# The second layer's pairs in a written order, with a second stage of seven block products

## The chip, the cores and the metric

The kernel runs on one core of a Trainium2 chip. The metric is the device time of one execution in microseconds (us); the time before is the median of three runs, 1736.29 us (1735.03 to 1740.18). The core has five instruction streams that matter here: TensorE (PE) multiplies, VectorE (DVE) and ScalarE (ACT) do elementwise work, GpSimd (POOL) helps in the attention layers, and SyncE (SP) issues the DMA transfers.

## What is computed

Four layers with residuals are applied to x, 2048 rows of 640 numbers: attention over a dilated window (layer A), a Fourier mixing layer (layer B), and both again.

```python
x = x + A(layernorm(x), wqkv, wo)
x = x + B(layernorm(x), seq_re, seq_im, hid_re, hid_im)
x = x + A(layernorm(x), wqkv, wo)
x = x + B(layernorm(x), seq_re, seq_im, hid_re, hid_im)

def B(x, Cr, Ci, Hr, Hi):      # 2048x2048 and 640x640
    a = x @ Hr.T
    b = x @ Hi.T
    return Cr @ a - Ci @ b
```

Only layer B is touched by the change, and above all its second use.

## The kernel before

Layer B is computed in the other order. The first stage multiplies the normalised x with the sequence matrices and gives, for a tile of 256 output rows, a real part Zr and an imaginary part Zi, held transposed: five chunks of 128 hidden columns, each with 256 rows of Zr and 256 of Zi. The second stage is y = Zr Wr + Zi Wi (the sign is in Wi), with contraction over the five chunks. There are eight such tiles, t = 0 to 7.

Every fp32 operand is split in a high part and the rest (hi and lo, both float32r), and every product is three matmuls (hi hi, hi lo, lo hi; `PASSES`). Splitting a coefficient tile (`s_split`) is a ScalarE copy (line 1327) and a VectorE subtraction (line 1328).

Tiles 1 to 6 are made in three pairs (`pair`, t1 = 2p + 2 and t2 = 2p + 3) that take seven block products in place of eight in the first stage. A pair is three sweeps over eight steps i. A step loads coefficient tiles of 128 x 512 numbers (256 KB; `s_raw`, line 1317) into seven buffers in turn (five of tag win, two of xa), forms sums and differences of them on VectorE (`combine`, line 1363), splits them into six split buffers (`views`), loads ready-made combinations of x (256 KB; `x_slot`, line 1307) into slots, and multiplies (`product`, line 1334). A block product of a step is six matmuls of 512 columns, a product with the fifth chunk three. So the first sweep has 18 matmuls and two x loads a step (m5, m4, m7), the second 21 and two (m2, f1, f2, f1, m1), the third 15 and one (m3, f2, m6). There are eight x slots in the first two sweeps and four in the third. Between the sweeps VectorE and ScalarE combine the eight PSUM banks' results into the pair's two tiles, `zt_put` splits a tile into four buffers (lines 1207, 1209, 1212), and `ymm` (line 1233) does the second stage for a row block of 128: per chunk and half of 320 columns, three passes for each of Zr and Zi, 60 matmuls for a row block and 120 for a tile. The row blocks of tile 2p + 1 stand at the end of the first and the second sweep, the first one of t1 inside the third sweep (12 matmuls a step from the fourth step on), its second one at the third sweep's end. Tiles 0 (in `run`) and 7 (after the last pair) are done apart. `yout` loads the residual rows, adds the two halves (line 1246) and stores (line 1253).

What sets the order: on TensorE it is the order in which the program is written, in both layers. The other engines of the pairs, SP's queue among them, are ordered by a scheduler that may move an instruction ahead of others that are written before it. Whatever stands behind a waiting instruction on one engine, or behind a waiting transfer on SP's queue, waits with it. `run` comes ahead of the pairs of each layer B: it does the first stage of tile 1, loads and splits the second stage's weights (`load_w`: wr and wi), and stores the combinations of x to DRAM (`x_combine`). In the first layer B the third pair is interleaved with the start of the next attention layer and has only the win buffers from its fourth step on.

## Time and profile before

| | before |
|---|---|
| median of three runs | 1736.29 us |
| profiled execution, first to last instruction | 1734.8 us |
| TensorE busy | 1715.3 us, 99% |
| VectorE busy | 1355.3 us, 78% |
| ScalarE busy | 824.7 us, 48% |
| DMA traffic | 419.91 MB, mean 242 GB/s |

The profiled execution has no time of its own but the span between its first and its last instruction, 1734.8 us; the median of the timed runs is 1.49 us above that span. The page of the profile gives busy time by engine and by groups of equal instructions. The chain of work that ended last follows the program back from its end, at each step to what released it. The waits list who stood idle until whom. In a window the columns are busy time of each engine with the number of its instructions, the granted clock of TensorE (1.00 is full), the share of the 16 DMA engines in use and the rate. In that profile layer B's pairs stand at about 457 to 868 us (first) and 1314 to 1707 us (second), each pair taking 133.3 us; the program ends with the second stage of the last tiles.

### The profile page before, as it was taken

The page shows a single profiled execution, that of the slowest core. Times are in us where ns is not written, and L with a number is a line of the kernel's source. Part 1 is how long each engine was busy: PE and PEld are TensorE (multiplying, and loading weights), DVE is VectorE, ACT ScalarE, POOL GpSimd, SP SyncE. Part 2 cuts the span into 40 slices and gives each one's busy share as a digit, 9 for nine tenths or more (in the row PEclk, how much of TensorE's full clock was granted, in tenths as well). Part 3 has the DMA queues.
Part 4 walks back from the last instruction along what each step waited for, and adds up shares of the span by engine and source line. Part 5 has one row for each costly group of instructions (what it writes and reads, how often), then busy time and mean ns, then how long its engine had stood idle before and what let it go on. Part 6 is the DMA issues. An engine that isn't in the chain of part 4 may idle for free.

```text
span 1734.8 us, 26552 instructions
## 1 busy us (share of the span) xinstructions
PE 1715.3 (99%) x8825; PEld 1496.1 (86%) x8825; DVE 1355.3 (78%) x2118; ACT 824.7 (48%) x1815; POOL 616.4 (36%) x570
## 2 busy tenths in 40 slices
PE   9999999999999999999999999999999999999999
PEld 7888888878888888888888889888888888888888
DVE  5999999978768667668639998899787677686673
ACT  5655645655445444445534434555444443443441
POOL 3899999940000000000019997899200000000000
PEclk9999999999999999999999999999999999999999
DMA  7768678959787687687547856698597867767761
GB/s 248 259 226 260 215 241 307 335 192 355 258 268 239 221 258 227 218 268 227 186 156 259 281 165 223 214 338 282 195 345 258 264 204 259 256 209 244 261 203 54
DMA packets 266713, 419.91 MB, mean 242 GB/s; under 512 B 22192, under 2 KB 144560, under 8 KB 266320
## 3 DMA queue, kind: packets, MB, share of 16 engines
q1 hardware_dynamic: 252400, 408.55, 71.2%
q10 hardware_dynamic: 14176, 9.67, 1.8%
q8 instruction: 70, 1.15, 0.3%
q14 instruction: 67, 0.55, 0.1%
HBM read 332.99 MB, written 85.14 MB: 241 GB/s over the span
## 4 chain that ended last, share of the span: by engine, by line
PE 86%; DVE 5%; POOL 3%; DMA 2%; issue 2%; ACT 2%; SPq 0%; DVEq 0%; ACTq 0%; POOLq 0%
PE m L499 18%; PE aux L1233 16%; PE t L1334 11%; PE m L1334 11%; PE aux L662 6%; PE pq L1334 6%; PE xt L1334 5%; PE m L1166 4%; PE t L1166 4%; PE xt L1166 2%; DVE pr L579 2%; DVE pr L622 1%; POOL pr L637 1%; POOL pr L582 1%; POOL pr L638 1%
## 5 line engine op out<-in xcount | busy, mean ns | idle before, releaser
L499 PE MATMUL m<-r,s 128*128 128x512 f32 (+1 forms) x1890 | 421.8, 378 | 0.2 <-ACT sg L514 0.2
L499 PEld LDWEIGHTS m<-r,s 128*128 128x128 f32 x1890 | 344.5, 188 | 54.7 <-ACT sg L514 1.6
L1327 ACT CAST r<-win 128x512 fp32r<-128x512 f32 x242 | 147.4, 621 | 168.2 <-DVE win L1363 80.4
L1233 PE MATMUL aux<-r2a,zo 128*128 128x320 f32 x768 | 226.0, 309 | 0.0
L579 DVE TENSOR_TENSOR pr<-pq,win 128x1280 f32<-128x1280 f32 x128 | 189.8, 1483 | 37.2 <-PE aux L1233 20.3
L637 POOL TENSOR_TENSOR pr<-pr 128x640 f32<-128x640 f32 x126 | 207.7, 1648 | 27.1 <-DVE pr L622 25.9
L1233 PE MATMUL aux<-pr,zo 128*128 128x320 f32 x704 | 208.0, 309 | 0.0
L582 POOL TENSOR_TENSOR pr<-pr 128x640 f32<-128x640 f32 x123 | 176.6, 1436 | 87.6 <-DVE pr L579 87.6
L622 DVE TENSOR_TENSOR pr<-pq,win 128x1280 f32<-128x1280 f32 x128 | 190.3, 1488 | 2.6
L1328 DVE TENSOR_TENSOR r<-win,r 128x512 fp32r<-128x512 f32 x242 | 162.7, 687 | 37.8 <-ACT r L1327 36.5
L300 POOL TENSOR_TENSOR stats<-stats,mhalf 128x1 f32<-128x1 f32 (+1 forms) x26 | 18.9, 728 | 445.9 <-ACT stats L294 445.9
L1334 PE MATMUL m<-r,r 128*128 128x512 f32 x600 | 153.0, 389 | 0.5 <-DVE r L1328 0.5
L1233 PEld LDWEIGHTS aux<-r2a,zo 128*128 128x128 f32 x768 | 144.1, 188 | 2.2
L1233 PEld LDWEIGHTS aux<-pr,zo 128*128 128x128 f32 x704 | 132.2, 188 | 2.4
L1334 PEld LDWEIGHTS m<-r,r 128*128 128x128 f32 x600 | 112.4, 188 | 24.0 <-DVE r L1328 1.0
L1334 PE MATMUL t<-r,r 128*128 128x512 f32 x492 | 132.0, 390 | 0.0
L638 POOL TENSOR_TENSOR pr<-pr 128x320 f32<-128x320 f32 x126 | 113.0, 897 | 9.9
L592 DVE TENSOR_REDUCE lg<-pr 128x64 f32<-128x640 f32 (+1 forms) x128 | 107.2, 837 | 11.4 <-POOL pr L582 11.3
L1363 DVE TENSOR_TENSOR win<-win,win 128x512 f32<-128x512 f32 x109 | 74.9, 691 | 49.9 <-DMA win<-cs_in 48.4
L1334 PEld LDWEIGHTS t<-r,r 128*128 128x128 f32 x492 | 92.4, 188 | 19.8
L1166 PE MATMUL m<-s,r 128*128 128x512 f32 x348 | 106.8, 395 | 1.7 <-ACT r L1103 0.9
L1166 PE MATMUL t<-s,r 128*128 128x512 f32 x348 | 105.2, 390 | 0.0
(299 smaller groups left out, 3245.6 us busy)
## 6 DMA issues: line engine op xcount, KB each, us to landing
win<-cs_in SPq DMA_DIRECT2D x346, 256.0 KB
r<-xc SPq DMA_DIRECT2D x240, 256.0 KB
win<-kvb SPq DMA_DIRECT2D x96, 440.0 KB
xa<-cs_in SPq DMA_DIRECT2D x120, 256.0 KB
win<-kvb SPq DMA_DIRECT2D x64, 360.0 KB
xc<-sg SPq DMA_DIRECT2D x28, 512.0 KB
xr<-xs SPq DMA_DIRECT2D x40, 320.0 KB
kvb<-stg SPq DMA_DIRECT2D x33, 320.0 KB
```

Of the source, the lines that this page charges most:

```text
L499: nc.tensor.matmul(mt[g][:, : GW[q]], st[:, a, k], wq[q][:, b, k], start=n == 0, stop=n == 14)
L579: nc.vector.tensor_tensor(pr, q, wview(u, jp, 0, [[1, FE]]), op=ALU.mult)
L582: nc.gpsimd.tensor_tensor(pv[:, :, 0:10], pv[:, :, 0:10], pv[:, :, 10:20], op=ALU.add)
L592: nc.vector.tensor_reduce(rows(lgs[u], jp), pv.rearrange("p (a h) d -> p a h d", h=HE), axis=AX.X, op=ALU.add,)
L622: nc.vector.tensor_tensor(pr.rearrange("p j w (h d) -> p (j w) h d", d=DH), rows(lgs[u], jp).unsqueeze(3).to_broadcast([P, 2 * W, HE, DH]) ...
L637: g.tensor_tensor(pr[:, :, 0:4], pr[:, :, 0:4], pr[:, :, 4:8], op=ALU.add)
L638: g.tensor_tensor(pr[:, :, 0:2], pr[:, :, 0:2], pr[:, :, 2:4], op=ALU.add)
L1166: self.last = nc.tensor.matmul(self.z[t][k], self.xn[c][:, a, j, k * P : (k + 1) * P], self.ct[s][:, b], start=s == 0 and i == 0, stop=s = ...
L1233: self.last = nc.tensor.matmul(self.ym[e][:, :320], zt[(k, a, ri)][:, j2 * P : (j2 + 1) * P], w[:, e * 320 : (e + 1) * 320], start=(k, a, ...
L1327: nc.scalar.copy(hi, raw)
L1328: nc.vector.tensor_tensor(lo, raw, hi.bitcast(F32), op=ALU.subtract)
L1334: nc.tensor.matmul(bank, w(a, kb), hl[b], start=start and (a, b) == (0, 0), stop=stop and (a, b) == (1, 0),)
```

## The change

In the first layer B:
- `pair` stores two of the third sweep's combined coefficient tiles of every step to DRAM (`keep`, into ccb), since the second layer uses the same ones.
- In the first two pairs, every other step of the first two sweeps makes one of 16 sums of second-stage weights (`v_make`: a VectorE sum, a split, a store of 320 KB into wvb; every fourth also loads two rows of weights of 320 KB).

In the second layer B:
- `run` also stores the first 256 columns of the x of eight row groups (`x_keep`, 256 KB each), so that the third sweep's m3 takes its x from a slot and the room in xn becomes free for weights.
- `pairs7` takes the place of the three calls of `pair` and of the two calls after them. All engines but GpSimd keep the written order. A step issues the coefficient loads two steps ahead, the x loads one step ahead, the pending stores and, in pair 0's second and third sweep, two loads of weight halves (160 KB each, 32 in all, `v_get`). There are four x slots throughout (`ring`), five split buffers, and the third sweep loads two ready-made tiles, so it has no combinations of its own, and two x loads a step. m6 accumulates on the banks of m1.
- For tiles 2 to 7 the second stage takes four of the five chunks as a 2 x 2 block product: rows are the two row blocks, the inner index is Zr or Zi, columns are the two halves of 320. Seven products of sums replace the eight; each is 12 matmuls (four chunks, three passes) and the fifth chunk is added plainly, six matmuls for each of the four results. `STAGES` is their order, with four PSUM chains of which three share one bank; after each stage VectorE adds the bank to half a residual row block (`v_stage`). `v_evac` makes the sums and splits in seven pieces, spread over the steps of the next sweep by `v_run`. Tile 1 still uses `ymm` and `yout`, written at the ends of pair 0's first two sweeps.

```diff
+STAGES = (
+    (3, ("a11", "r0"), None, (0, 0)),
+    (0, ("a12", "i0"), (0, 0), (0, 0)),
+    (3, ("s2", "t2"), None, (0, 1)),
+    (1, ("s1", "t1"), None, (1, 1)),
+    (1, ("s4", "i1"), (0, 1), (0, 1)),
+    (3, ("s3", "u"), None, (1, 0)),
+    (2, ("a22", "t4"), (1, 0), (1, 0)),
+    (3, None, (1, 1), (1, 1)),
+)
...
+        def x_keep(self, i):
+            c, j = divmod(i, NJ)
+            nc.sync.dma_start(self.xc[3][:, i], self.xn[c][:, :, j, 0:256].bitcast(F32))
...
+        def v_make(self, i):
...
+            nc.vector.tensor_tensor(o, a, b, op=op)
+            hl = T([P, 2, 320], "wa", F32R)
+            nc.scalar.copy(hl[:, 0], o)
+            nc.vector.tensor_tensor(hl[:, 1], o, hl[:, 0].bitcast(F32), op=ALU.subtract)
+            nc.sync.dma_start(wvb[:, x, n], hl.bitcast(F32))
...
+            def sums(raw, hi, lo, dg, ks):
+                a11, a21 = raw[:, :, 0, 0:P], raw[:, :, 0, P:]
+                a12, a22 = raw[:, :, 1, 0:P], raw[:, :, 1, P:]
+                v.tensor_tensor(a22, a21, a22, op=ALU.add)
+                v.tensor_tensor(a21, a21, a11, op=ALU.subtract)
+                v.tensor_tensor(a11, a11, a22, op=ALU.subtract)
+                v.tensor_tensor(a12, a12, a11, op=ALU.add)
...
+            parts = [(whole, x) for x in plain] + [(direct, g) for g in groups]
+            for g in groups:
+                parts += [(sums, g), (halves, g)]
+            return parts
...
+        def v_flush(self):
+            for dst, src in self.pend:
+                nc.sync.dma_start(dst, src)
+            self.pend = []
+
+        def v_stage(self, t, n, tags=("aux0",) * 3 + ("aux1",)):
+            chain, prod, plain, (j, e) = STAGES[n]
+            start = (t, chain) not in self.vb
+            if start:
+                self.vb[(t, chain)] = pt([P, 512], tags[chain])
+            bank = self.vb[(t, chain)]
...
+            for i, (l, r) in enumerate(mms):
+                nc.tensor.matmul(
+                    bank[:, :320], l, r, start=start and i == 0, stop=i == len(mms) - 1, skip_group_check=not start
+                )
+            h = self.half[(j, e)]
+            nc.vector.tensor_tensor(h, bank[:, :320], h, op=ALU.add)
...
+        def pairs7(self):
+            v, act = nc.vector, nc.scalar
+            ring = [(c, j) for c in range(2) for j in range(NJ)][4:]
...
+            views = cells + ["s0", "s1"][:1]
...
+            for n, (p, sw, i) in enumerate(steps):
...
+                load(n + 2)
+                fifo += atoms(n + 2)
+                loadx(n + 1)
+                self.v_flush()
+                if p == 0 and sw > 0:
+                    for _ in range((0, 2, 2)[sw]):
+                        if gets:
+                            self.v_get(*gets.pop(0))
+                fill()
...
+                    if fast:
+                        self.v_stage(tp, 0)
+                        fill(2)
+                        self.v_stage(tp, 6)
+                    else:
+                        self.ymm(tp, 0, 0, KD)
+                        fill(2)
+                        self.yout(tp, 0, None)
...
+                    if fast:
+                        for k, st in enumerate((2, 3, 5, 4, 7)):
+                            self.v_stage(tp, st)
+                            if k in (2, 3):
+                                fill(1)
+                    else:
+                        self.ymm(tp, 1, 0, KD)
+                        fill(2)
+                        self.yout(tp, 1, None)
...
+                    if 3 <= i < 6:
+                        self.v_stage(t1, (1, 0, 6)[i - 3])
...
+            for n in (1, 0, 6, 2, 3, 5, 4, 7):
+                self.v_stage(t, n, ("m0", "m1", "aux0", "aux1"))
+                self.v_flush()
...
             def ahead_c(i):
                 b12, b22, b11 = raw(t2, i), raw(t2, NP + i), raw(t1, i)
                 x6 = self.x_slot(6, i, ring)
-                c3 = split(combine(b22, b12, b22, ALU.subtract))
-                return x6, c3, split(b12), lambda: split(combine(b11, b11, b12, ALU.add))
+                keep(i, 0, combine(b22, b12, b22, ALU.subtract))
+                c3 = split(b22)
+
+                def rest():
+                    keep(i, 1, combine(b11, b11, b12, ALU.add))
+                    return split(b11)
+
+                return x6, c3, split(b12), rest
...
+            if self.seven:
+                with tc.manual_schedule(engines=ENGINES - {nc.gpsimd.engine}):
+                    self.pairs7()
+                return
             for p in range(NPAIR - (nstats is not None)):
                 self.pair(p, nstats)
 
@@ -1536,8 +2013,6 @@
     b1.run(st2)
     layer_a(2, st2, b2, b1)
     b2.run(None)
-    b2.ytile(NT - 1, 0, None)
-    b2.y_final(NT - 1)
```

More of the change, by code (lines that the diff above doesn't have):

```diff
@@ L1077, in __init__ @@
             self.late = []
+            self.seven = li == 3
+            self.todo = []
             self.nraw = self.nhl = self.nx = self.nc_ = 0
@@ L1416, in pair @@
                     self.product(m7, x7, c7, *ends)
+                    if i % 2 == 0 and 8 * p + i // 2 < 4 * len(KS):
+                        self.v_make(8 * p + i // 2)
                     self.tick()
@@ L1512, in run @@
                     self.z_mm(s, None, 1)
+                    if self.seven and 4 <= s < 4 + NP:
+                        self.x_keep(s - 4)
                     self.tick()
```

341 lines of the change are left out of this document (340 added, 1 removed).

## The prediction

> **What bounds the kernel now.** I read the page first, then the waits of TensorE, then the chain of work that ended last, and only then the queues.
>
> ```profile
> span 1734.8 us, 26552 instructions
> PE 1715.3 (99%) x8825; PEld 1496.1 (86%) x8825; DVE 1355.3 (78%) x2118; ACT 824.7 (48%) x1815; POOL 616.4 (36%) x570
> ```
>
> TensorE is busy nearly all the span, so removed matmuls shorten the program only by as much as TensorE then finds no new wait. The stretch that the change rewrites is the second spectral layer, 1315 us to the end. Its waits, of the matmuls and of the weight loads ahead of them, were asked for on their own:
>
> ```profile
> PE xt L1334 <- DVE r L1328: 0.2, 1, 0.2
> PEld xt L1334 <- DVE r L1328: 0.6, 1, 0.6
> PEld t L1334 <- ACT r L1327: 0.5, 1, 0.5
> ```
>
> That is all: some 420 us with three waits of under a microsecond. There is nothing to win there but instructions, and any lateness that the new order brings is a pure loss. What an instruction is worth is read from the chain of that stretch (start, length, what):
>
> ```profile
> 1325.88 1.36 PE m L1334 x6
> 1329.96 1.36 PE m L1334 x6
> 1332.83 5.59 DMA xa<-cs_in
> 1346.77 8.79 PE aux L1233 x60
> 1358.31 1.36 PE m L1334 x6
> 1363.07 1.36 PE m L1334 x6
> 1393.67 8.79 PE aux L1233 x60
> 1421.27 1.75 PE aux L1233 x12
> 1426.45 1.75 PE aux L1233 x12
> 1703.38 28.19 PE aux L1233 x192
> ```
>
> Sixty matmuls of the second stage (L1233) take 8.79 us, 146.5 ns each; the page's mean for one of them is longer, because matmuls overlap. The other rows give the step lengths of the three sweeps: 4.08 us for the 18 matmuls of the first sweep (1325.88 to 1329.96), 4.76 us for the 21 of the second (1358.31 to 1363.07), and 5.18 us less the 1.75 us of second-stage work, 3.43 us, for the 15 of the third. The last 192 matmuls run without a gap.
>
> **What is removed.** A tile had 5 chunks x 2 halves x 2 row blocks x 6 = 120 matmuls. Now four chunks go in seven products of 4 x 3 = 12 matmuls, and the fifth stays plain with 24: 108. Tiles 0 and 1 keep the old form, so six tiles save 12 each: 72 x 146.5 ns = 10.55 us. This is the whole gain; the number of first-stage matmuls doesn't change. The Trainium skill ("TensorE: Matmul & The Clock Gate", Back-to-back issue gap) gives a warm matmul N/2.4 + 2.5 ns, which is 135.8 ns for 320 columns and would make the saving 9.8 us; the chain shows 146.5 ns, and the measurement decides.
>
> That the new operands cost the same is bounded by rows of the first stage, whose moving operand lies in two separate runs (r) or in one piece (s):
>
> ```profile
> L1334 PE MATMUL m<-r,r 128*128 128x512 f32 x282 | 71.7, 389 | 0.0
> L1334 PE MATMUL m<-s,r 128*128 128x512 f32 x144 | 36.7, 389 | 0.0
> ```
>
> No difference; I take none for weights that lie in four runs of 80.
>
> **VectorE, and the tail.** The rows for the pair from 1448 us:
>
> ```profile
> L1328 DVE TENSOR_TENSOR r<-win,r 128x512 fp32r<-128x512 f32 x38 | 25.3, 686 | 6.2 <-ACT r L1327 6.1
> L1363 DVE TENSOR_TENSOR win<-win,win 128x512 f32<-128x512 f32 x18 | 12.3, 690 | 3.9 <-DMA win<-cs_in 3.6
> L1246 DVE TENSOR_TENSOR xr<-aux,xr 128x320 f32<-128x320 f32 x8 | 3.7, 486 | 2.6 <-PE aux L1233 2.6
> L1212 DVE TENSOR_TENSOR zo<-s,zo 128x256 fp32r<-128x256 f32 x5 | 2.0, 418 | 0.0
> ```
>
> A tile's operands now take one subtraction of 512, and for each of two groups one of 256 and one of 512, four sums of 256 and one subtraction of 1024: 0.69 + 2 x (0.42 + 0.69 + 4 x 0.42 + 2 x 0.69) = 9.0 us, where five of 0.69 us were enough (3.5 us). Two combinations a step (0.69 us each) go from the third sweep, since the first layer leaves them in memory. A third-sweep step then needs 3 x 0.69 = 2.1 us of 3.43; the first sweep still 5 x 0.69 = 3.5 of 4.08, and it carries the 9.0 us of pieces over six steps with a slack of 6 x 0.6 + 2.6 (18 second-stage matmuls) = 6.2 us. The 2.8 us over come out of the lead of five split buffers (five products of six matmuls, 1.36 us each). Cost nothing, and if that cover is gone, 2.8 us a pair. At the end there is no next sweep to hide under: after the last product VectorE has two combinations (1.4), the pieces (9.0) and five additions (5 x 0.49 = 2.4), 12.8 us, while TensorE has 60 matmuls (8.8) and then 18 of the next tile on another bank (2.6). Price 12.8 - 11.4 = **1.4 us**; 0 if the operations overlap a little, 3 if they wait for ScalarE's copies.
>
> **The SP queue, where I expect most of the gain to go.** All transfers stand in one written order on SP. A step issues three coefficient loads two steps ahead, two x loads one step ahead (four slots instead of eight), then stores. The second-stage output of tile 1 still goes the old way (L1246, L1253): its store stands on SP behind the additions, so what is written after it waits until TensorE has finished 60 matmuls. The trace of before shows the same block:
>
> ```profile
> 1351.95 0.33 SPq L1317 DMA_DIRECT2D win<-cs_in  x1
> 1356.12 0.34 SPq L1253 DMA_DIRECT2D y_out<-xr  x1
> ...
> 1407.52 0.33 SPq L1317 DMA_DIRECT2D win<-cs_in  x1
> 1407.94 0.39 SPq L1307 DMA_DIRECT2D r<-xc  x1
> ```
>
> SP issues nothing from 1351.95 until the store at 1356.12, 0.56 us after TensorE has gone on (1346.77 + 8.79 = 1355.56). Before, eight slots held the next steps; now the x of step 1 is written behind that store and three loads. With 0.42 us from issue to issue (1407.52 to 1407.94) it is issued 0.56 + 4 x 0.42 = 2.2 us after TensorE resumes. How long it takes to land lies between the wait that a load into an idle queue ended, and the 5.59 us in the chain above:
>
> ```profile
> 1410.44 0.69 DVE L1363 TENSOR_TENSOR win<-win,win 128x512 f32<-128x512 f32 x1 [1.75 <-DMA win<-cs_in]
> ```
>
> (1407.52 to 1410.44, 2.9 us). What a transfer takes of the DMA engines is in the sizes and in the windows (last two columns: share of the engines, GB/s):
>
> ```profile
> win<-cs_in SPq DMA_DIRECT2D x51, 256.0 KB
> r<-xc SPq DMA_DIRECT2D x40, 256.0 KB
> ```
>
> ```profile
> 734.00:736.00 2.00, 2.00 (x11) 1.65 (x10) 0.72 (x2) 0.00 (x0) 0.00 (x0) 1.00 1.02 378
> 738.00:740.00 2.00, 2.00 (x11) 1.65 (x10) 1.87 (x4) 1.56 (x3) 0.00 (x0) 1.00 1.08 383
> 1448.80:1480.00 31.20, 31.20 (x139) 25.81 (x138) 22.64 (x39) 13.26 (x23) 0.00 (x0) 1.00 0.85 276
> 544.50:583.00 38.50, 38.50 (x195) 33.44 (x194) 25.80 (x45) 16.14 (x31) 2.10 (x2) 1.00 0.59 191
> 1260.00:1270.00 10.00, 10.00 (x54) 8.85 (x53) 9.49 (x14) 5.66 (x10) 0.00 (x0) 1.00 1.02 382
> 1300.00:1310.00 10.00, 10.00 (x57) 9.02 (x57) 6.01 (x9) 3.04 (x7) 0.00 (x0) 1.00 0.71 258
> ```
>
> With a backlog 380 GB/s, 0.69 us for 256 KB; by the long window 276/0.85 = 325 GB/s, 0.81 us. I take 380, since a late queue has a backlog. Four transfers in front, served 0.69 apart but issued 0.42 apart, add 1.1 us: the x lands 2.2 + 2.9 + 1.1 = 6.2 us after TensorE resumes.
> - Pair 0, second sweep: needed after 4.76 us. **1.4 us** late (0.4 to 3.1).
> - Pair 0, third sweep: needed after 3.43 us. **2.8 us** late (1.7 to 4.4). Then each step moves five transfers of 256 KB and two weight fetches of 160 KB, 1.64 MB: 4.31 us at 380 GB/s for a step of 3.43. Two more steps pass before second-stage work (48 matmuls, 7.0 us) gives time back: 2 x 0.9 = **1.8 us** (0 to 4.3).
> - Pairs 1 and 2: the stores are written one step later, behind the next x, and the x after it is needed after 2 x 3.43 = 6.9 us. **0.5 us** each (0 to 1.8).
>
> In the first sweep a step of 4.08 us holds five transfers (3.45 us), and after second-stage work the x behind the stores is needed only after two steps, 8.2 us: nothing there.
>
> **The first layer.** Each third-sweep step gets two stores of 256 KB, 16 x 256 KB in 38.5 us, on top of 191 GB/s: 300 GB/s. In its first three steps six transfers (4.1 us) stand against 3.43, 0.7 us a step, under a lead of six split buffers. **1.0 us** for the layer, 0 to 3 x 2.1 = 6.4. The weight sums (in two pairs a sweep gets four stores and two loads of 320 KB, 63 GB/s beside 276) fit under 380 and are put at nothing, up to 2.8 us at 325. Eight stores of 256 KB go into a stretch already at 382 GB/s (1260 to 1270), but 1300 to 1310 stands at 0.71: nothing, at most 8 x 0.69 = 5.5 us.
>
> **The sum.** -10.55 + 1.4 + 1.4 + 2.8 + 1.8 + 2 x 0.5 + 1.0 = -1.15 us, on the profiled span 1734.8 - 1.15 = 1733.65. The median of the runs, 1736.29, lies 1.49 us above that span; carried over, **1735.1 us**: no change that can be measured (0.3%, about what a measurement of this kernel can tell from none, is 5.2 us).
>
> **The rivals.**
> - *The transfers come in time.* Only the tail is lost: -9.15 us, 1727.1. For it: two-microsecond windows at 378 and 383 GB/s with TensorE busy throughout. Against it: the block on SP is in the trace of before, and only its eight slots made it harmless. Any result faster by over 0.3% needs less than 5.3 us of the 9.4 us of losses: chance 0.27.
> - *The DMA engines become the bound, and it is slower.* Place: the third sweeps of both layers. At 325 GB/s pair 0 loses 1.9 + 3.3 + 4.3, pairs 1 and 2 three steps of 0.6 us each (3.6), the first layer 6 x 0.81 x 8 = 38.7 us against 3 x 3.43 + 5 x 5.18 = 36.2 in three sweeps (7.5) and 2.8 for the weight sums; with the tail 24.8 - 10.55 = +14.2, 1750.5. Between 9.4 us of losses at 380 and 24.8 at 325, the 15.8 us that make it measurably slower are reached near 357 GB/s. For it: every long window has a share and rate of that ratio. Against it: the short windows. Chance 0.23. The Trainium skill ("DMA: Bandwidth & Descriptors", Specifications) puts the memory's limit for a core at about 358 GB/s, which would end at this rival's edge; the windows above 378 disagree with it. The same table asks for 512 B and more per piece, and 18 of the 32 weight fetches land in pieces of 320 B; if that doubled them (an estimate by that page; no run here shows it), pair 0 would lose up to 18 x 0.44 = 7.9 us more.
> - *The change saves no time on TensorE.* If weights in four runs made a matmul 163 ns long, 108 would take what 120 did, and with the losses it were +9.4 us, 1745.7. The two rows of r and s speak against it. Chance 0.03.
>
> **How the numbers follow.** No change 0.47, faster 0.27, slower 0.23 + 0.03. The range leaves out the far end of each rival: 1728.5 (losses of 2.8 us) to 1746 (losses of 20.3 us).
>
> **What would show it.** In the profile after: second-stage matmuls in groups of 12 and 18 at 146 ns, 72 fewer; in pair 0, waits of TensorE's first product of the second and third sweeps for the x loads (L1307's tiles), some 1 and 3 us, and none of that kind at the first sweep; a DMA share near 1 in that third sweep; one wait of under 2 us on the accumulating bank in the last 27 us. Wrong would be: waits for splits on VectorE instead of x, stalls spread evenly over all pairs (then the rate is the bound), or over 3 us of new idle time before 1315 us.

## The result, and the profile after

The changed kernel takes **1762.07 us** (median of 4 runs, 1760.44 to 1763.35) against 1736.0 us of the kernel before on the same chip: a ratio of 1.0143 (95% interval 1.0129 to 1.0157), 26.1 us slower. The forecast was 1735.1 us with a range of 1728.5 to 1746, so the result lies outside the range.

The first lines of the page after, and its waits of TensorE (us in total, times, longest):

```profile
span 1761.6 us, 26765 instructions
PE 1719.9 (98%) x8753; PEld 1487.2 (84%) x8753; DVE 1374.9 (78%) x2168; ACT 835.5 (47%) x1836; POOL 618.7 (35%) x570
```

```profile
PE xt L1573 <- DMA r<-xc: 11.7, 10, 5.4
PE pq L364 <- DVE s L375: 3.0, 2, 1.5
PE aux L1451 <- DVE xr L1455: 2.8, 2, 1.7
PE aux L1451 <- DVE qs L1455: 2.3, 1, 2.3
```

The 72 matmuls are gone (8825 - 8753). Where the second layer's pairs had three waits of under a microsecond, they now have ten for x loads (r<-xc), up to 5.4 us; the row of L364 lies ahead of these pairs. The second-stage matmuls cost what the prediction said; this is the chain of the changed kernel in a stretch of pair 1 (start, length, what):

```profile
1575.33 2.63 PE aux L1451 x18
...
1581.39 1.75 PE aux L1451 x12
```

That is 146 ns each. The chain of the same kernel where pair 0's second sweep starts, and where its third does:

```profile
1363.21 0.69 PE xt L1573 x3
1363.90 0.69 PE t L1573 x3
1364.60 0.68 PE pq L1573 x3
1365.28 0.42 PE t L1573 x2
1365.69 4.16 DMA r<-xc
1369.86 0.14 issue
1369.99 0.93 PE xt L1573 x3
```

```profile
1418.37 6.15 DMA r<-xc
1424.52 0.14 issue
1424.66 1.62 PE xt L1573 x3
```

And SP's queue behind the first of the two (start, time until the issues are done, line, transfer):

```profile
1363.77 0.35 SPq L1268 DMA_DIRECT2D y_out<-xr  x1
1364.21 0.38 SPq L1775 DMA_DIRECT2D win<-cs_in  x1
1364.69 0.40 SPq L1775 DMA_DIRECT2D xa<-cs_in  x1
1365.18 0.42 SPq L1775 DMA_DIRECT2D win<-cs_in  x1
1365.69 0.90 SPq L1765 DMA_DIRECT2D r<-xc  x2
```

This is the order the prediction described: a store that waits for the additions, three loads, then the x of the next step, issued 2.5 us after TensorE resumed (1363.21) and landing 4.16 us later.

A table of the second layer's pairs shows how much each stretch takes (from here on, "the second layer takes" means from the start of its pairs to the end of the program). A stretch runs from the start of its first product to the start of the next stretch's first product, so it holds the second-stage work at its end; the last ends with the last matmul. All times are us, read from the timelines of TensorE; the three columns on the right belong to experiments below.

| stretch | before | changed | late stores | x first | order and banks |
|---|---|---|---|---|---|
| the pairs start at | 1313.11 | 1321.41 | 1315.07 | 1319.59 | 1321.19 |
| pair 0, first sweep | 42.29 | 41.64 | 41.46 | 41.71 | 44.13 |
| pair 0, second sweep | 46.91 | 52.63 | 49.54 | 47.29 | 46.90 |
| pair 0, third sweep | 46.28 | 54.67 | 49.39 | 57.21 | 45.28 |
| pair 1 | 133.29 | 135.70 | 135.54 | 137.27 | 132.52 |
| pair 2 and the last tile | 149.68 | 152.35 | 149.97 | 151.21 | 148.81 |

So 8.3 us are lost ahead of the pairs and 18.5 from there on. Two things stand between these differences and the real losses. Since 12 matmuls a tile went (one tile in pair 0's third sweep, two in pair 1, three at the end: 1.8, 3.5 and 5.3 us), the new rows ought to be shorter. And in the kernel before the first six matmuls of pairs 1 and 2 stand inside the row above theirs (pair 1's at 1438.40 to 1440.84), 1.4 us that belong to the next row. So the real losses are 16.6 us in pair 0, 5.9 in pair 1 and 6.6 in the last row.

One thing stood in no step of the prediction: the granted clock halves after the waits. These are windows of the changed kernel (busy time and count of each engine, then clock, DMA share, GB/s), the first two being whole second and third sweeps of pair 0:

```profile
1363.20:1407.10 43.90, 40.96 (x171) 32.35 (x170) 25.59 (x40) 19.49 (x33) 0.00 (x0) 0.96 0.95 300
1415.90:1470.60 54.70, 46.67 (x230) 39.66 (x229) 33.46 (x58) 17.91 (x29) 0.00 (x0) 0.94 0.88 288
1372.00:1374.00 2.00, 2.00 (x6) 1.61 (x5) 0.21 (x1) 0.62 (x1) 0.00 (x0) 0.50 1.02 352
1426.00:1428.00 2.00, 2.00 (x6) 1.54 (x5) 0.00 (x0) 0.36 (x1) 0.00 (x0) 0.50 1.09 357
```

And the loss of 8.3 us ahead of the pairs is eight times the 1.0 us that the first layer's additions were given.

### The profile page after: what moved, and what is told of

Read it like the earlier page. It is cut to its first block, busy times and chain, and to the rows that moved or that the text cites. A ratio compares the mean times of both kernels' runs of the same rounds, so it can differ in the third digit from the quotient of the medians.

```text
span 1761.6 us, 26765 instructions
## 1 busy us (share of the span) xinstructions
PE 1719.9 (98%) x8753; PEld 1487.2 (84%) x8753; DVE 1374.9 (78%) x2168; ACT 835.5 (47%) x1836; POOL 618.7 (35%) x570
## 4 chain that ended last, share of the span: by engine, by line
PE 74%; DMA 11%; DVE 9%; ACT 3%; issue 2%; POOL 0%; SPq 0%; ACTq 0%; DVEq 0%; POOLq 0%
PE m L512 22%; PE aux L1248 7%; PE aux L675 6%; PE t L1573 4%; PE aux L1451 4%; DMA win<-cs_in 4%; PE m L1792 4%; PE m L1573 4%; PE t L1792 4%; DMA r<-xc 3%; PE xt L1573 3%; PE m L1181 3%; PE t L1181 2%; PE pq L1573 2%; PE pq L1792 2%
## 5 line engine op out<-in xcount | busy, mean ns | idle before, releaser
L592 DVE TENSOR_TENSOR pr<-pq,win 128x1280 f32<-128x1280 f32 x128 | 189.8, 1482 | 38.6 <-PE aux L1248 20.3
L313 POOL TENSOR_TENSOR stats<-stats,mhalf 128x1 f32<-128x1 f32 (+1 forms) x26 | 22.8, 879 | 448.2 <-ACT stats L307 448.2
L1248 PE MATMUL aux<-r2a,zo 128*128 128x320 f32 x480 | 141.4, 309 | 0.0
L1518 ACT CAST r<-win 128x512 fp32r<-128x512 f32 x135 | 83.1, 621 | 108.4 <-PE pq L1573 24.9
L1248 PE MATMUL aux<-pr,zo 128*128 128x320 f32 x440 | 130.1, 309 | 0.0
L1519 DVE TENSOR_TENSOR r<-win,r 128x512 fp32r<-128x512 f32 x135 | 92.0, 688 | 38.5 <-ACT r L1518 37.1
L1785 ACT CAST r<-win 128x512 fp32r<-128x512 f32 x126 | 76.2, 619 | 84.7 <-DVE win L1821 58.3
L1786 DVE TENSOR_TENSOR r<-win,r 128x512 fp32r<-128x512 f32 x126 | 85.0, 688 | 22.1 <-ACT r L1785 21.4
L526 ACT COPY stg<-m 128x480 f32<-128x480 f32 x96 | 53.6, 559 | 98.0 <-PE m L512 91.5
L1573 PE MATMUL m<-r,r 128*128 128x512 f32 x360 | 92.1, 391 | 0.0
L1248 PEld LDWEIGHTS aux<-r2a,zo 128*128 128x128 f32 x480 | 90.1, 188 | 1.4
L1248 PEld LDWEIGHTS aux<-pr,zo 128*128 128x128 f32 x440 | 82.6, 188 | 1.6
L675 PE MATMUL aux<-r2a,ot 128*128 128x320 f32 x540 | 83.7, 310 | 0.0
```

The lines of the kernel that those rows point to most:

```text
L592: nc.vector.tensor_tensor(pr, q, wview(u, jp, 0, [[1, FE]]), op=ALU.mult)
L675: nc.tensor.matmul(m[:, :320], oT[(c, j)][:, a, k], wo_s["w"][:, b, k, e * 320 : (e + 1) * 320], start=(i, k) == (0, 0), stop=(i, k) == (2 ...
L1248: self.last = nc.tensor.matmul(self.ym[e][:, :320], zt[(k, a, ri)][:, j2 * P : (j2 + 1) * P], w[:, e * 320 : (e + 1) * 320], start=(k, a, ...
L1573: nc.tensor.matmul(bank, w(a, kb), h[b], start=start and (a, b) == (0, 0) and not cont, stop=stop and (a, b) == (1, 0), skip_group_check=cont,
```

## The experiments

Theory A: the written order of SP (and of VectorE) makes x, splits and additions late, and the clock falls after the waits. Rival B: the DMA engines are full in pair 0 (0.95 and 300 GB/s in the row above), so whatever order one writes, the bytes set the time. For the first layer: is it the added stores, by their bytes or by their place in a queue, or only a shifted schedule? "Over before" is the difference of the medians to the kernel before in the same comparison; the changed kernel itself stands at 26.1.

**Stores behind x.** In pair 0, the two stores of tile 1 are put on the list that is flushed behind the next x loads:

```
-                        self.yout(tp, 0, None)
+                        self.yout(tp, 0, None, 1)
+                        self.pend += [x[1:] for x in self.late]
+                        self.late = []
...
```

> The changed kernel with one edit: in pair 0 of the second layer the stores of tile 1's two finished y tiles are written on SP behind the x loads of the next sweep, not ahead of them. Theory A (the order written on SP makes x late, and the granted clock falls to about 0.5 after that wait): the 2.0 us wait for x at 1369.99 and the 5.5 us wait at 1424.66 go, and with them the matmuls at half clock (about 2.1 and 2.6 us): 8 to 12 us less than the 1762.1 of the change, about 1750 to 1754. Theory B (the DMA engines are full in pair 0 at 300 to 317 GB/s, so what is not lost in x is lost in the raw loads and splits): at most 3 us less, 1759 to 1762, with the idle time moved to the splits and the raw loads.

Measured: 1756.73 us (1745.92 to 1761.2), 19.8 over before, ratio 1.0104 (1.0069 to 1.0139). In the profiled run (1745.92) the second layer takes 11.2 us less than in the changed kernel (1744.1 - 1315.07 = 429.0, against 1761.6 - 1321.41 = 440.2), as A said: 3.1 of them in pair 0's second sweep and 5.3 in its third. The longest wait for x there falls from 5.4 to 2.2 us, with the engines as full as in the third sweep of the changed kernel (0.88 and 288 GB/s above):

```profile
1406.10:1455.00 48.90, 44.87 (x226) 38.82 (x226) 33.06 (x57) 17.78 (x29) 0.00 (x0) 0.97 0.89 296
```

But the median moved by 6.3 us only, to between the ranges of A and B, and the runs are 15 us apart. That profiled run also starts the pairs 6.3 us earlier than the changed kernel, so a part of the spread lies in the first layer, which this edit doesn't touch.

**Weights spread.** Pair 0's weight pieces over three sweeps:

```
-                if p == 0 and sw > 0:
-                    for _ in range((0, 2, 2)[sw]):
+                if p == 0:
+                    for _ in range((1, 2, 1)[sw]):
```

> The changed kernel with pair 0's weight pieces fetched in the ratio 1, 2, 1 per step over its three sweeps in place of 0, 2, 2, so that the third sweep moves less. Theory A (x late by the written order, then a low clock): 0 to 2 us less, 1760 to 1762, as the x loads stand where they stood. Theory B (full DMA engines): the third sweep's rate drops below the 317 GB/s and with it most of the wait of 5.5 us for x and the 1.8 us of late splits: about 4 us less, 1757 to 1759.

Measured: 1760.21 us (1757.77 to 1765.59), 23.3 over before, ratio 1.0138 (1.0116 to 1.016). The window of the third sweep with its second-stage work in this run:

```profile
1417.00:1469.50 52.50, 46.21 (x231) 39.93 (x230) 33.20 (x57) 18.03 (x29) 0.00 (x0) 0.93 0.83 275
```

The share over the whole stretch is down to 0.83, and TensorE still waits 4.7 us for x at 1425.28; the time is the one that A gave. But the mean of 52 us doesn't show how full the engines were while that x was under way. First the changed kernel, from the issue of its x to the end of the wait, then this run:

```profile
1418.40:1424.50 6.10, 0.87 (x4) 0.38 (x2) 2.58 (x5) 2.06 (x4) 0.00 (x0) 0.83 0.94 283
```

```profile
1419.70:1425.10 5.40, 0.90 (x4) 0.40 (x3) 2.61 (x5) 2.06 (x4) 0.00 (x0) 0.83 0.91 287
```

There the engines were nearly full in both, at some 285 GB/s, so this run alone doesn't rule B out for that wait. What speaks against B in the third sweep is the run with late stores: the same bytes, another order, and less than half the wait.

**x first.** The x loads of the next step ahead of the raw loads of the step after it:

```
+                loadx(n + 1)
                 load(n + 2)
                 fifo += atoms(n + 2)
-                loadx(n + 1)
```

> The changed kernel with the next step's x loads written on SP ahead of the raw coefficient load of the step after it, in all pairs. Theory A: the second sweeps of pairs 1 and 2, which lose 2.2 to 2.5 us each, and parts of the third sweeps get that back, as x no longer stands behind a load that waits for its buffer: 6 to 8 us less in pairs 1 and 2 and up to 4 in pair 0, about 1750 to 1755. Theory B (bytes): no change, or up to 3 us more, since the raw load then starts later: 1762 to 1765.

Measured: 1759.52 us (1755.95 to 1760.48), 22.6 over before, ratio 1.0125 (1.011 to 1.014). The total lies in neither range, and the table shows what it hides. Pair 0's second sweep falls from 52.63 to 47.29 us, and the second sweeps of pairs 1 and 2, 40.7 and 40.4 us of products in the changed kernel, to 38.26 and 38.27, as before. In the changed kernel SP's raw loads, with x behind them, had stood still for VectorE in pair 1's second sweep (us in total, times, longest):

```profile
SPq L1775 <- DVE win L1514: 10.7, 5, 4.0
```

The second sweep of pair 0 in the run with x first:

```profile
1361.30:1399.90 38.60, 38.46 (x171) 31.57 (x170) 25.47 (x38) 18.66 (x30) 0.00 (x0) 1.00 1.03 336
```

Share 1.03 at 336 GB/s, and TensorE busy for 38.46 of 38.60 us: the engines carry all the bytes of that sweep in time if x is asked for first. This is the row that decides for A in the second sweeps. But the third sweeps lose what was won, at a place that neither theory named (timeline of VectorE at the end of pair 0, with the idle time before an instruction and what ended it):

```profile
1446.66 0.69 DVE L1514 TENSOR_TENSOR xa<-win,xa 128x512 f32<-128x512 f32 x1 [1.88 <-DMA xa<-cs_in]
...
1456.08 1.28 DVE L1514 TENSOR_TENSOR stg<-m,stg 128x512 f32<-128x512 f32 x2
1457.27 0.48 DVE L1455 TENSOR_TENSOR xr<-aux,xr 128x320 f32<-128x320 f32 x1
```

VectorE works on the next pair's raw coefficients, now loaded later, ahead of this pair's sums; the addition at 1457.27 is late, and with it the stage that waits for its bank (4.0 us at 1457.81).

**Waits filled.** Matmuls without use ahead of the two products that wait, to see whether the half clock comes from standing idle and what it costs:

```
+            def idle(count, r):
+                bank = pt([P, 512], "aux0")
+                for _ in range(count):
+                    nc.tensor.matmul(bank, self.x_plain(0, 0, 512)(0, 0), r, start=True, stop=True)
...
+                    if p == i == 0:
+                        idle(20, hl[(n, "c3")][0])
                     product(bk["m3"], x[0], h("c3"), *ends)
```

> The changed kernel with matmuls without use (8 ahead of pair 0's second sweep, 20 ahead of its third, 128x512 like the products) in the two waits for x of 2.0 and 5.4 us, so that TensorE is not idle there; no other edit. If the granted clock of 0.5 behind these waits comes from TensorE standing idle: the clock stays at 1.0 there, and the 2.1 and 2.6 us of slow matmuls go: 1756 to 1759. If it has another cause (DMA load, for one): the clock falls as before and the time is 1761 to 1764.

Measured: 1760.5 us (1760.01 to 1763.52), 24.2 over before, ratio 1.0137 (1.012 to 1.0154). The same two stretches as above, and the waits of TensorE in the second layer:

```profile
1372.00:1374.00 2.00, 2.00 (x11) 1.64 (x10) 0.16 (x2) 0.65 (x2) 0.00 (x0) 1.00 0.92 272
1426.00:1428.00 2.00, 2.00 (x11) 1.59 (x9) 0.92 (x3) 1.25 (x2) 0.00 (x0) 1.00 1.05 384
```

```profile
PE xt L1578 <- DMA r<-xc: 6.1, 9, 1.3
```

The clock stays at 1.00, so idleness was the cause. The time is above the 1756 to 1759 expected, and its runs overlap with those of the changed kernel (24.2 over before against 26.1), so by the medians the half clock cost some 2 us at most: with full speed the products only reach the next late x sooner (new waits of 0.85 at 1429.18 and 0.96 at 1433.78). The part of theory A that counted the slow matmuls as a loss of 2.1 and 2.6 us falls here.

**Order mended.** Late stores and x first together, and in the last step of a third sweep no split of the next pair ahead of the sums:

```
+                if sw == 2 and i == NP - 1:
+                    while (n, "c6") not in hl:
+                        fill(1)
+                else:
+                    fill()
...
                     self.v_run(9)
+                    fill(2)
```

> The changed kernel with three edits to its written order and none to its work: tile 1's stores behind the x loads (as in the run with late stores), x loads ahead of the raw loads of the step after (as in the run with x first), and in the last step of a third sweep the next pair's splits behind the sums that the y stages wait for. Theory A (the loss in the second layer is the written order): the second layer's part falls from 440 us to 420 or less (late stores took 11.2 off, x first 2.3 each off two second sweeps and 1.6 off two third sweeps, and the 4.8 us that x first lost at the third sweeps' ends should go): about 1742 to 1748. Theory B (the DMA engines are full): what x gains the raw loads lose, 1753 to 1758.

Measured: 1747.32 us (1745.46 to 1750.19), 11.0 over before, ratio 1.0063 (1.0048 to 1.0078): within what A gave, outside B's. The second layer takes 1745.3 - 1317.67 = 427.6 us, not the 420 hoped for; its waits:

```profile
PE aux L1451 <- DVE xr L1455: 4.4, 3, 2.0
PE aux L1451 <- DVE qs L1455: 2.3, 1, 2.3
PE xt L1573 <- DMA r<-xc: 1.7, 1, 1.7
PE aux L1451 <- DMA r2a<-wvb: 1.2, 1, 1.2
```

The added fill(2) stood ahead of an addition that the stages need, and 2.3 us are the last tile's bank, which an earlier stage's addition still reads.

**Order and banks.** So the next edits move that fill behind the second y stage, spread the weight pieces, and give the last tile other banks:

```
-                        elif k in (2, 3):
+                        elif k in (1, 2, 3):
...
-                self.v_stage(t, n, ("m0", "m1", "aux0", "aux1"))
+                self.v_stage(t, n, ("m0", "m1", "xt", "t0"))
```

> The changed kernel with the mended order (x loads ahead of the raw loads, tile 1's stores behind them), and with three more edits: at a third sweep's end the next pair's splits behind the second of the five y stages, not behind the sums alone; pair 0's weight pieces at 1, 2 and 1 per step over the three sweeps; and the last tile's four chains in banks that no stage before them uses. Theory A (the rest of the second layer's loss is order too): against the 1747.3 of the mended order, 2.3 us less at the last tile (the wait at 1727.12), 1 to 1.8 each at the ends of pairs 0 and 1 (the waits at 1450.07 and 1585.80), 1.2 to 2.9 in pair 0's third sweep (the weight piece at 1447.07 and x at 1418.42): 1738 to 1742. If pair 0 is held by its bytes, the last term stays: 1742 to 1744.

Measured: 1742.74 us (1738.68 to 1746.47), 6.2 over before, ratio 1.0032 (1.0022 to 1.0043). All of the 20 us between the changed kernel and this one are order, banks and the place of the weight fetches: no computation was removed and no byte saved. Its second layer takes 1742.0 - 1321.19 = 420.8 us where before took 1734.8 - 1313.11 = 421.7. The median is 0.7 us above A's range and inside the one given for a pair 0 that is held by its bytes. In the table the second and the third sweep of pair 0, which had lost most, are back at 46.90 and 45.28; the first sweep, which now shares the weight pieces, is 2.4 us longer than with the order alone (44.13 against 41.78). That the pieces cost this is not shown: with the same pieces the same sweep takes 42.25 and 42.02 us in two later runs (the mended order with the stores on ScalarE's queue, and with thin stores). The last tile still waits 1.9 us, now for an addition of its own chain.

**The first layer's additions alone.** The second layer of before, with the changed kernel's extra stores, which nothing reads (the changed kernel holds the old code of a pair too, and is sent back to it):

```
             def keep(i, n, raw):
+                if self.seven:
+                    return
...
-            if self.seven:
-                with tc.manual_schedule(engines=ENGINES - {nc.gpsimd.engine}):
-                    self.pairs7()
-                return
```

> The kernel before, with the changed kernel's additions to the first layer alone (the kept x slices and the ready-made weight combinations written to HBM, 19.9 MB of extra stores); the second layer is that of before and reads none of them. If these stores cost what the first layer lost in the changed kernel (second layer's start at 1321.57 instead of 1313.26): 5.7 to 8.3 us over the before, 1742 to 1744. If the loss came from the hand-over to the written order and not from the stores: within 2 us of the before, 1734 to 1738. The prediction's own term was 1.0 us.

Measured: 1744.9 us (1741.22 to 1745.55), 8.0 over before, ratio 1.004 (1.0026 to 1.0055). The stores are it, and not the hand-over. How much they cost differs from one execution to the next: with the same first layer the second layer's pairs start at 1315.07 to 1321.41 us in the table, where before has 1313.11. The next two runs split them; one leaves out the weight combinations (here), the other the store in keep:

```
-                    if i % 2 == 0 and 8 * p + i // 2 < 4 * len(KS):
-                        self.v_make(8 * p + i // 2)
...
```

> The kernel before with only the kept coefficient combinations (48 stores of 256 KB in the first layer) and the kept x slices, without the ready-made weight combinations; its second layer is that of before and reads none of them. The run with both additions cost 8.0 us (1744.9 against 1736.9). If the loss goes with the bytes (12.6 MB here of 19.9): about 5 us, 1741 to 1743. If it is the weight combinations that fill pair 0 of the first layer (all 16 ran there, 335 GB/s in its second sweep where before had 190): 1 to 3 us, 1737 to 1740.

> The kernel before with only the ready-made weight combinations (16 makes, 32 loads and stores of 320 KB or less in the first layer) and the kept x slices, without the kept coefficient combinations. By bytes (5.2 MB of stores and 2.6 MB of loads): about 3 us, 1739 to 1741. If pair 0's full DMA engines are the whole loss: 5 to 7 us, 1742 to 1744, and before's times in pairs 1 and 2 of the first layer.

Measured: the kept sums 1741.25 us (1736.83 to 1745.35), 4.9 over before, ratio 1.0027 (1.0017 to 1.0037); the weights 1738.45 us (1736.86 to 1741.68), 2.1 over before, ratio 1.0012 (1.0003 to 1.0022). 4.9 + 2.1 is near the 8.0 of both. The kept sums came out as the bytes would have it, the weights below both of their ranges. (The profile of the kept sums is of their fastest run, 1736.83 us; its pairs start at 1313.14, so it doesn't show the loss.) Where both stand, pair 0's second sweep and pair 1's third sweep of the first layer look like this, and in the kernel before like that:

```profile
496.90:537.70 40.80, 39.36 (x172) 31.40 (x171) 29.43 (x52) 21.71 (x44) 0.00 (x0) 1.00 0.92 317
679.70:721.00 41.30, 38.90 (x193) 33.12 (x193) 27.12 (x47) 14.95 (x30) 2.08 (x2) 1.00 0.77 258
```

```profile
497.50:535.70 38.20, 38.20 (x171) 31.63 (x170) 26.78 (x42) 21.07 (x38) 0.00 (x0) 1.00 0.82 262
677.80:716.80 39.00, 38.46 (x192) 33.08 (x192) 26.35 (x47) 15.05 (x30) 2.14 (x2) 1.00 0.61 198
```

So pair 0's second sweep went from 262 to 317 GB/s, not from 190 to 335 as the expectation of the kept sums has it.

Bytes or the place in the queue? In the run of the kept sums alone, their stores cut to 16 of 512 columns, or whole from ScalarE's queue:

```
-                nc.sync.dma_start(ccb[:, p, i, n], raw.rearrange("p r t -> p (r t)"))
+                nc.sync.dma_start(ccb[:, p, i, n, 0:16], raw[:, 0, 0:16])
```

> The same kernel with the 48 stores on SP's queue and each cut to 16 of its 512 columns (8 KB in place of 256), so that their number and what they wait for stay and the bytes go; the kept sums are stored in part only, and nothing reads them. If the bytes cost: within 1.5 us of before, 1736 to 1738. If the place on SP's queue costs: 1740 to 1742.5, as with the whole stores.

```
-                nc.sync.dma_start(ccb[:, p, i, n], raw.rearrange("p r t -> p (r t)"))
+                nc.scalar.dma_start(ccb[:, p, i, n], raw.rearrange("p r t -> p (r t)"))
```

> The kernel before with the kept coefficient combinations and x slices stored in the first layer, as in the run of the kept sums alone, but with the 48 stores of the sums issued from ScalarE's queue in place of SP's; the second layer is that of before. If their cost (4.9 us, 1741.25 against 1736.32) is loads held up behind them on SP: 0 to 2 us over before, 1736 to 1738.5. If it is the bytes: as with SP, 1740 to 1742.5.

Measured: thin 1736.97 us (1735.01 to 1739.57), 0.7 over before, ratio 1.0004 (0.9995 to 1.0012); from ScalarE's queue 1744.14 us (1740.06 to 1747.97), 7.9 over before, ratio 1.0042 (1.0028 to 1.0055). With thin stores, as many and behind the same waits, the loss is gone: it is the size of the stores and not their place on SP. (A thin store also lets go of its buffer sooner; what of the size acts through the engines and what through the buffers was not taken apart.) Off SP's queue the loss doesn't go either; that it is 3 us larger there, above both ranges, is not explained. The second edit in the kernel with order and banks:

> The changed kernel with the mended order, spread weight pieces and free banks (1742.74), and the kept sums' stores on ScalarE's queue. If the stores cost by their place on SP: about 4 us less, 1738 to 1740, still at or over the 1736.5 of before. If by their bytes: no difference, 1741 to 1744.

Measured: 1741.58 us (1740.81 to 1744.24), 5.3 over before, ratio 1.0031 (1.002 to 1.0042): no difference from 6.2.

**Without the kept sums.** Can the second layer add them itself? On VectorE, then on GpSimd (its lines are shown), from the kernel with order and banks; two of the four runs also make the weight combinations one pair later:

```
-                    raws[n] = [pre(p, i, 0), self.s_raw(t2, i, wide), pre(p, i, 1)]
+                    raws[n] = [self.s_raw(*a, wide) for a in ((t2, NP + i), (t2, i), (t1, i))]
...
+                    nc.gpsimd.tensor_tensor(b22, b12, b22, op=ALU.subtract)
...
+                    nc.gpsimd.tensor_tensor(b11, b11, b12, op=ALU.add)
...
-                    if i % 2 == 0 and 8 * p + i // 2 < 4 * len(KS):
-                        self.v_make(8 * p + i // 2)
+                    if i % 2 == 0 and 0 <= 8 * p + i // 2 - 8 < 4 * len(KS):
+                        self.v_make(8 * p + i // 2 - 8)
```

> The same with the kept coefficient combinations given up: the first layer doesn't store them (12.6 MB less), and the second layer's third sweeps add them on VectorE again, two additions of 0.69 us a step, from raw loads as many as before. Run alone, these stores cost 4.9 us (1741.25 against 1736.32). If VectorE has room in the third sweeps: 5 us less than the run beside it, 1733 to 1737, level with or below the before. If VectorE's additions make the splits late (11 us more of VectorE in a sweep of some 43 us): no gain, 1738 to 1745.

> As the run without kept sums, with the 16 weight combinations of the first layer written for its pairs 1 and 2 in place of 0 and 1. Alone they cost 2.1 us (1738.45 against 1736.32), in pair 0's second sweep (40.2 us in place of 38.3). If that is because pair 0 already moves more than the others: 1 to 2 us less than the run without kept sums, 1731 to 1736. If the planner's order of the engines, or the first layer's end, takes it back: the same within 1 us or up to 3 us more.

> The changed kernel with the mended order, spread weight pieces and free banks (1742.74), without the kept coefficient combinations: the third sweeps of the second layer add them on GpSimd, two additions of 128x512 a step, where GpSimd takes 1.4 to 1.7 us for one of 128x640 in the kernel before. If the first layer's loss was the bytes, and GpSimd's additions (some 2.6 us in a step of 5.2) come in time: about 5 us less, 1736 to 1739, level with the before at 1736.3. If the longer way to the splits (load, sum, split) makes these late: 1740 to 1746.

> The same with the first layer's weight combinations written for its pairs 1 and 2 in place of 0 and 1. If their 2.1 us come from pair 0's load: 1 to 2 us less than the run beside it, 1734 to 1738. If they come wherever they are put: the same within 1 us.

Measured: on VectorE 1750.45 us (1748.02 to 1754.31), 13.9 over before; with the weights later 1750.71 us, 14.2 over. (In these two the difference of a step has the other sign, b22 - b12, so they don't compute the layer; the instructions are the same in number and size.) On GpSimd 1763.58 us (1757.89 to 1764.64), 26.6 over; with the weights later 1763.05 us, 26.1 over. All four lie above every time that was given; that the place of the weights makes less than 1 us of difference was one of the two outcomes named for it. VectorE has no room: its run waits for the additions of the stages,

```profile
PE aux L1451 <- DVE xr L1455: 6.7, 4, 3.4
```

and GpSimd's sum stands between the load and ScalarE's copy; VectorE waits behind that in its order, and TensorE waits 2.8 us for one split:

```profile
PE m L1583 <- DVE r L1519: 7.3, 4, 2.8
```

So the kept sums are worth their bytes: added by VectorE instead, the kernel is 7.7 us slower on balance (13.9 against 6.2 over before).

**Do the two losses add up?** The kept sums' stores thin, raw loads of the same size in place of reading them back, in the mended kernel and in the changed one:

```
-                nc.sync.dma_start(raw.rearrange("p r t -> p (r t)"), ccb[:, p, i, n])
+                nc.sync.dma_start(raw.rearrange("p r t -> p (r t)"), cs[2 * p + 2 + n][:, i, :])
```

> The mended kernel (order, weight pieces, banks: 1742.74) with the kept sums' stores cut to 16 of 512 columns; in their place the second layer's third sweeps load raw coefficients of the same size, so that two of its products a step are taken of other data than the reference's. If the bytes of these stores cost 4.9 us there too: 1737 to 1739, the time of before. If the first layer's time hangs on something else that the runs of the stores alone had in common: 1741 to 1744.

> The changed kernel itself (1762.07) with the same edit: stores of the kept sums cut to 16 of 512 columns, raw coefficients of the same size loaded in their place, two products a step taken of other data. If the two losses add up: about 5 us less, 1756 to 1758, so that some 20 us over before stay with the second layer. If the second layer's loss grows out of the first's (late data that it reads back): 1745 to 1752.

Measured: 1738.26 us (1736.45 to 1742.25), 2.9 over before, ratio 1.0017 (1.0008 to 1.0026), and 1758.79 us (1757.96 to 1759.89), 23.4 over before, ratio 1.0134 (1.012 to 1.0148). Against 6.2 and 26.1 over before, both are about 3 us better, where 5 were expected (the first lies in its range even so, the second 0.8 us above). For the mended kernel this is clear; for the changed one the two intervals overlap (1.0120 to 1.0148 and 1.0129 to 1.0157), but its trace agrees that the losses add up: without the bytes its second layer takes 1756.2 - 1315.59 = 440.6 us, with them 440.2. So the second layer's loss does not grow out of the first's. No version of the change that computes the whole reference came below the kernel before.

## Why the prediction was wrong, step by step

By the profiles (spans of 1761.6 and 1734.8 us) the losses were 26.8 + 10.55 = 37.4 us where 9.4 were forecast: 16.6 in pair 0 (6.0 forecast), 12.5 in pairs 1 and 2 with the tail (2.4), 8.3 ahead of the second layer's pairs (1.0). Most of it came from the order in which the transfers and splits were written: order, banks and the place of the weight fetches alone took 19.9 us off the changed kernel.

- **"72 x 146.5 ns = 10.55 us"**: right. 72 matmuls fewer, 146 ns each in the chain after.
- **"Pair 0, second sweep: 1.4 us late"**: right in mechanism, too small. The wait was 2.0 us at 1369.99, and x landed 6.6 us after TensorE resumed where 6.2 was worked out. But the stretch lost 5.7 us: the step priced one late x as if the next ones were on time. With four slots each x is asked for one step ahead, behind raw loads that wait for buffers, so nothing gives the time back. Asking for x first won back nearly all of it.
- **"Pair 0, third sweep: 2.8 us late" and "1.8 us" for the rate**: 4.6 us forecast, and with the tile's removed matmuls and the next pair's six 11.5 lost (54.67 - 46.28 + 1.8 + 1.4). The landing was mis-sized: 6.15 us from issue, not 2.9 + 1.1, and the wait 5.4. While that x was under way the engines moved 283 GB/s at a share of 0.94, not the 380 that were put in; over whole sweeps they had 300 and 336 at 0.95 and 1.03. The rate alone didn't decide it, since with the stores written later the same bytes went with a wait of 2.2; why this x took so long to land is open.
- **"Pairs 1 and 2: 0.5 us each"**: the step that failed outright. They lost 5.9 and 6.6 us, tail included. It looked only at the stores; by the written order x also stood behind a raw load whose buffer is free only after the step's fourth split (2.4 and 2.2 us in the second sweeps, shown by x first), and VectorE's splits for the next pair stood ahead of the sums (waits of 1.1 to 1.7 us).
- **"Price 1.4 us" for the tail**: 2.3, for another reason: a bank that a former stage's addition reads. With other banks a wait of 1.9 for an addition of the tile's own chain took its place, the kind that the prediction had meant.
- **"1.0 us for the layer" (the first)**: 8.0 measured alone; the pairs start 8.3 us later, past the 3 us named as a sign of being wrong. It set the weight sums at nothing and let 380 GB/s with a lead of six split buffers hide the rest. The step's upper ends, 6.4 + 2.8, hold the result.
- **The rivals.** "The DMA engines become the bound" gave 1750.5, nearest of all, and its first-layer part (7.5 + 2.8) was near the 8.0. Its second-layer part had the wrong mechanism. The sign given for it, "stalls spread evenly over all pairs", misled: a fault in a written order is repeated in every pair as well. The other two are out.
- **Not foreseen**: the half clock, which by the medians cost some 2 us at most.

Open: with order, banks and bytes mended the second layer still takes 1736.4 - 1318.62 = 417.8 us, 3.9 less than before and not 10.55. The waits that its view lists sum to some 4 us; the rest was not taken apart. Open too is why the stretch behind the first layer's pairs, up to those of the second, is longer in the run of the stores alone (440.2 us, 437.5 before). The eight stores of x (`x_keep`) are issued there, but they are in the runs of the thin stores and of the kept sums as well, where that stretch takes 437.7 and 437.5. A version with fewer bytes kept was not tried.

## What to carry to other kernels

When slots are cut and an order is written by hand, follow each transfer through all the steps until the slack is back, not only to the first late one: ask what stands ahead of it in its queue and what that waits for, in every stage and not only where a store blocks. Data kept by an early stage for a later one is paid in the early stage in bytes; thin stores (same count, few columns) show that price in one run. And where a wait ends in slow matmuls, fill it once before blaming the clock: the next late transfer may take the time anyway.

## What the runs showed of the hardware

- A wait of TensorE of 2.0 us, up to 1369.99, was followed by a granted clock of 0.50 (still 1.00 at 1370.50 to 1371.00, 0.50 from 1371.50 to 1374.50), one of 5.4 us by 0.50 over 1424 to 1428; filled with useless matmuls both stayed at 1.00. The Trainium skill ("TensorE: Matmul & The Clock Gate", Part 1: The HAM clock gate) says that the clock goes to half after an idle window of about 3.4 us. The half agrees with the rows; that 2.0 us of waiting can be enough does not follow from it.
- 336 GB/s at a share of 1.03 was carried over a whole sweep (38.6 us) with TensorE busy all but 0.14 us. A high DMA share alone is no proof of a bound.
- GpSimd added 128x512 in 1.29 us and up to 1.6 in the mean of a group, where VectorE takes 0.69, and a split of VectorE beside it took 1.11 in place of 0.68 (run with the sums on GpSimd):

```profile
1556.47 1.29 POOL L1557 TENSOR_TENSOR win<-win,win 128x512 f32<-128x512 f32 x1
```

```profile
1557.20 1.11 DVE L1519 TENSOR_TENSOR r<-xa,r 128x512 fp32r<-128x512 f32 x1 [3.62 <-ACT r L1518]
1558.23 0.68 DVE L1519 TENSOR_TENSOR r<-win,r 128x512 fp32r<-128x512 f32 x1
```
